# A two-stage kernel (RWKV-style attention, then a squared-ReLU MLP): one hand-held list that orders all engines and transfers is replaced by another

## The chip, the cores and the metric

The kernel runs on one NeuronCore of one Trainium2 chip. The metric is the device time of one execution in microseconds (us). The kernel before takes 181.06 us, the median of 3 runs (181.05 to 181.49). Engine names in the profile: PE is TensorE's matmul, PEld its weight load, DVE VectorE, ACT ScalarE, POOL GpSimd, SP SyncE, which issues all DMAs here.

## What is computed

Inputs are r, k, v, w of shape (4 batches, 8 heads, 768 tokens, 48), u of (8, 48), and two weight matrices. The reference, cut down:

```
for t in range(768):                       # attention, per batch b and head h
    y[t]  = r[t] @ (state + outer(u * k[t], v[t]))
    state = w[t][:, None] * state + outer(k[t], v[t])
x = y.transpose(0, 2, 1, 3).reshape(3072, 384)
h = x @ w_in                               # 384 -> 2048
g = maximum(h, 0) ** 2
out = g @ w_out                            # 2048 -> 384, float32
```

## The kernel before

**Tiling.** The 4 x 768 tokens are cut into 12 steps of 256 tokens (3 steps for a batch; the state is carried inside a batch). Each step has two chunks of 128 tokens. For each step s the kernel does an attention part and an MLP part; an operation's name in the list carries the step and then its part, so `m1_.4.7` is the eighth piece of the first MLP matmul of step 4.

**Attention part of step s.** Four loads, `ld.s.w`, `.k`, `.r`, `.v` (384 KB each, L178). `ww_` multiplies the decays of two neighbouring tokens (L264), `lw_` takes the logarithm on ACT (L268), `cum_` sums logarithms on PE into the PSUM tile `att` (L324 to L328), `al_` (DVE, L333) makes the second sum out of the first in steps 3 to 11, `exp_` and `ac_` exponentiate on ACT (L340, L346). `rw_`, `kw_`, `ku_`, `qp_` prepare products of r, k, w, u (L286, L290, L297, L302), `q_` is a DVE reduction (L307), `qs_`, `v_`, `vs_` are casts and moves (L277, L272). `rd_.s.0` and `rd_.s.1` (DVE, L358 and L361) write the decayed r and k into `rdec_buf` and `kdec_buf`. Their transposes rT and kT are made in steps 0 to 3 by PE (`tr_`, L374) with a copy by DVE or ACT (`rkt_`, L389 and L391), and from step 4 on by a DMA transpose (`dtr_`, L398 and L401). `p_` is the score matmul (L418), `pm_` its masking on DVE (L429 where the scores lie in two single banks, L432 where they lie in an `att` tile), `su_`, `ts_`, `sn_` make the next state (PE L444, DVE or ACT L452/L454, POOL L459), `y_` and `yc_` are the output matmuls (L481, L491), `vq_` (L316) and `ysb_` (DVE, L502) finish y. `yt_` with `xt_` (PE L514, then a copy, L519), or a DMA transpose `dyt_` (L523), give the transposed input xT of the MLP.

**MLP part of step s.** `m1_.s.0` to `.7` (PE, L534) are six matmuls each, into one of four PSUM banks (`bk` 0 and 1, `m1` 0 and 1; the number behind the colon). `rl_` (ACT L543 or DVE L545) empties the bank with ReLU into `gt`; `sq_` squares four pieces at a time (ACT L551 or DVE L553). `m2_.s.c.q` (PE, L562) are four matmuls that add into one bank per chunk c, `os_` (ACT L569 or DVE L571) empties it, `store.s.c` writes 192 KB out (L575). The weights come in eight loads of 768 KB, `ld.0.i` to `ld.3.i` for w_in (L188) and `ld.0.o` to `ld.3.o` for w_out (L194), and are cast to bf16 by `cast.i.*` and `cast.o.*` (L200) on ACT, DVE or POOL.

**What sets the order.** A single string, `ORDER`, of 865 words. The kernel walks it from front to back, and each word issues its instructions; nothing is reordered after that, so each engine's queue, and SP's queue of DMAs, is the string with the other engines' words left out. A word says which engine does the operation where there is a choice (`=A`, `=V`, `=G` for ACT, DVE, POOL) and which PSUM bank it gets (behind the colon). Dependencies between engines, and the reuse of buffers and banks, become semaphore waits; an engine that waits holds everything behind it in its queue. Buffers are few: 4 of each raw input, 4 stage buffers for weights, 3 of `gt`.

`warm_.n.b` issues n matmuls of 512 columns on zeros (L579) that nothing reads; there are 46 of them, all before the first `m1_`.

Of the kernel before, what the change touches and what calls it, by code (L numbers as in the profile page):

```python
# [22 lines left out]
rkt_.1.1=A vs_.1.0=A lw_.2 v_.1=G y_.0:0 yc_.0.1 p_.1.1:1 p_.1.0:m warm_.6.1 vq_.0=G pm_.1.1 cum_.2:1 vs_.1.1=A
pm_.1.0 qs_.1=A exp_.2 warm_.4.1 su_.1:m kw_.2=G ysb_.0=V rw_.2=G ts_.1.0=V y_.1:0 rd_.2.1 yc_.1.0 rd_.2.0
yt_.0:1 xt_.0=V sn_.1.0 cast.i.1=A vq_.1=G ts_.1.1=V tr_.2.1:2 yc_.1.1 ld.2.v tr_.2.0:0 m1_.0.3:1 rkt_.2.1=A
m1_.0.2:2 ac_.2 ysb_.1=V yt_.1:3 rkt_.2.0=A sn_.1.1 p_.2.1:1 rl_.0.3=A cast.i.0=V p_.2.0:0 xt_.1=A ku_.2=V
m1_.0.1:0 vs_.2.1=G m1_.1.0:3 m1_.1.2:1 vs_.2.0=A rl_.0.1=A m1_.1.1:0 v_.2=G rl_.0.2=A rl_.1.0=A rl_.1.2=A
qp_.2=G pm_.2.1 pm_.2.0 su_.2:1 rl_.1.1=V ts_.2.0=V ld.2.i m1_.0.0:2 m1_.1.3:1 cast.i.2=A y_.2:1 q_.2 yc_.2.0
sn_.2.0 yc_.2.1 rl_.1.3=A m1_.0.5:3 ld.3.i m1_.1.5:1 ld.3.w m1_.0.4:0 rl_.0.0=A rl_.0.5=V qs_.2=A rl_.1.5=A
cast.i.3=G m1_.1.7:3 ld.0.o m1_.1.4:1 vq_.2=V ysb_.2=V rl_.0.4=A rl_.1.7=A ww_.3=G cast.o.0=G m1_.0.7:2 yt_.2:3  # L30
ld.2.o m1_.0.6:0 lw_.3 cast.o.2=G cum_.3:1 xt_.2=V rl_.0.7=V ld.3.o m1_.2.4:3 rl_.0.6=V sq_.0.1=A ld.1.o
sq_.0.0=A rl_.1.4=A m1_.2.2:2 sq_.0.2=A m1_.1.6:0 m1_.2.7:1 ld.3.r rl_.1.6=A sq_.1.1=A rl_.2.2=V rl_.2.4=V
m1_.2.5:2 rl_.2.7=V ld.3.k al_.3 rl_.2.5=V cast.o.1=V m1_.2.6:0 m2_.0.1.0:3 m2_.0.1.2 sq_.1.3=V kw_.3=G
m1_.2.3:1 sq_.1.0=A ld.3.v ld.5.w m2_.0.0.0:2 ac_.3 ld.4.w ld.4.r sq_.0.3=A rl_.2.6=A exp_.3 vs_.3.1=G ld.4.v
ld.4.k m1_.2.0:0 m2_.0.0.2 m2_.0.1.1 cast.o.3=V rl_.2.0=A m1_.2.1:0 rw_.3=V m2_.0.1.3 sq_.2.3=A rl_.2.1=A
sq_.1.2=A rl_.2.3=A rd_.3.0 m2_.0.0.1 os_.0.1=A tr_.3.0:0 rd_.3.1 m2_.0.0.3 tr_.3.1:1 ku_.3=V m2_.1.0.1:3
os_.0.0=A m2_.1.0.0 rkt_.3.0=V rkt_.3.1=V p_.3.0:0 v_.3=G sq_.2.1=A su_.3:1 sq_.2.2=A vs_.3.0=A qp_.3=V ld.5.k
p_.3.1:b ts_.3.0=A m2_.2.0.1:2 m2_.1.0.3 m2_.2.0.3 m2_.1.0.2 sq_.2.0=A ww_.4=G pm_.3.0 lw_.4 q_.3 qs_.3=A
cum_.4:0 m2_.2.0.0 ld.6.w v_.4=A pm_.3.1 ww_.5=G rw_.4=G sn_.3.0 ts_.3.1=V vq_.3=G ac_.4 al_.4 m2_.2.0.2
yc_.3.1:1 y_.3 m2_.2.1.0:1 m2_.2.1.2 os_.1.0=A kw_.4=V lw_.5 ysb_.3=V sn_.3.1 store.0.0 os_.2.0=A exp_.4 kw_.5=G  # L40
rd_.4.1 rd_.4.0 cum_.5:1 ac_.5 yt_.3:3 vs_.4.1=G xt_.3=A ld.5.r vs_.4.0=A al_.5 store.0.1 ld.6.r m2_.2.1.3
m2_.2.1.1 os_.2.1=V m1_.3.0:3 rl_.3.0=A exp_.5 su_.4:0 m1_.3.1:2 rl_.3.1=A m2_.1.1.3:0 m2_.1.1.1 dtr_.4.1
ku_.4=V qp_.4=V rw_.5=V m1_.3.7:2 rl_.3.7=A m1_.3.6:1 ts_.4.0=V dtr_.4.0 rl_.3.6=A m2_.1.1.2 m1_.3.5:3 rd_.5.1
rl_.3.5=A m1_.3.4:1 sn_.4.0 ts_.4.1=V p_.4.0:0 q_.4 rd_.5.0 qs_.4=A ww_.6=G vq_.4=G rw_.6=G p_.4.1:1 sq_.3.0=V
m2_.3.1.0:3 m2_.1.1.0 pm_.4.0 yc_.4.1:0 yc_.4.0 sq_.3.3=A m1_.3.3:2 rl_.3.4=A sq_.3.2=A pm_.4.1 y_.4 lw_.6
m1_.3.2:1 rl_.3.3=A rl_.3.2=A cum_.6:1 m2_.3.0.2:2 m2_.3.0.3 sq_.3.1=A m2_.3.1.3 m2_.3.1.1 ku_.5=G qp_.5=G
ld.5.v ysb_.4=V al_.6 ld.7.w ld.6.k ww_.7=G yt_.4:1 m2_.3.1.2 m2_.3.0.0 exp_.6 ac_.6 os_.1.1=V sn_.4.1 m2_.3.0.1
kw_.6=V rd_.6.0 rd_.6.1 dtr_.5.1 ld.6.v v_.5=G dtr_.5.0 xt_.4=A p_.5.1:1 store.2.0 ld.7.r vs_.5.1=A os_.3.1=A
lw_.7 su_.5:b p_.5.0:0 q_.5 v_.6=A store.2.1 ts_.5.0=V m1_.4.1:1 ku_.6=G rl_.4.1=A vs_.6.0=A m1_.4.3:0 os_.3.0=A
pm_.5.0 pm_.5.1 rl_.4.3=V m1_.4.2:3 rl_.4.2=A vs_.6.1=A qs_.5=G m1_.4.4:1 sn_.5.0 yc_.5.1:0 yc_.5.0 rl_.4.4=V  # L50
su_.6:1 dtr_.6.0 m1_.4.7:3 rl_.4.7=A vs_.5.0=G dtr_.6.1 y_.5 m1_.4.6:1 ts_.6.0=V sn_.6.0 ld.9.w m1_.4.5:3
m1_.4.0:2 vq_.5=V sq_.4.1=A rl_.4.6=A rl_.4.5=A sq_.4.2=A ysb_.5=V ts_.6.1=V rl_.4.0=V sq_.4.0=V yt_.5:0
m2_.4.1.1:1 xt_.5=A qp_.6=G q_.6 qs_.6=G ld.7.k p_.6.0:1 ld.8.v yc_.6.1:0 ld.7.v ld.8.r p_.6.1:m store.1.1
ld.8.w vq_.6=G ku_.7=G pm_.6.1 sq_.4.3=A kw_.7=G m2_.4.1.0 m2_.4.1.2 m1_.5.1:0 rl_.5.1=A pm_.6.0 m2_.4.1.3
sn_.6.1 m1_.5.0:2 cum_.7:1 y_.6 m1_.5.7:3 vs_.7.0=A rl_.5.0=A os_.4.1=A ww_.9=V al_.7 m2_.4.0.0:0 rl_.5.7=V
m1_.5.2:2 m1_.5.6:1 ww_.8=G rw_.7=G exp_.7 ac_.7 m2_.4.0.1 vs_.7.1=G m2_.4.0.2 m1_.5.3:3 rl_.5.2=A sq_.5.0=A
v_.7=A rl_.5.3=A m1_.5.5:2 sq_.5.1=A ysb_.6=V vs_.8.0=G m2_.4.0.3 lw_.8 rl_.5.6=A rd_.7.1 qp_.7=V rd_.7.0
sq_.5.3=A su_.7:0 v_.8=G rl_.5.5=V rw_.8=V m1_.5.4:3 rl_.5.4=V m2_.5.1.0:2 cum_.8:1 sq_.5.2=A ts_.7.0=V al_.8
q_.7 m2_.5.1.1 m2_.5.1.3 store.1.0 ld.8.k ld.11.k ac_.8 store.3.1 dyt_.6 dtr_.7.1 dtr_.7.0 exp_.8 kw_.8=V
sn_.7.0 ts_.7.1=V m1_.6.2:3 m2_.5.1.2 m1_.6.3:1 ld.9.r ld.10.w sn_.7.1 os_.4.0=A rd_.8.1 m1_.6.1:0 os_.5.1=A  # L60
ku_.8=G m1_.6.7:2 rd_.8.0 rl_.6.2=V ld.9.k rl_.6.3=A qs_.7=A m1_.6.4:1 su_.8:1 rl_.6.7=A p_.7.1:m p_.7.0:0
qp_.8=G rl_.6.1=V ts_.8.0=V yc_.7.1:1 yc_.7.0 rl_.6.4=A sq_.6.1=A m2_.5.0.2:0 m1_.6.6:1 store.3.0 rl_.6.6=A
sq_.6.3=A dtr_.8.1 pm_.7.1 pm_.7.0 lw_.9 dtr_.8.0 m2_.5.0.1 m1_.6.5:2 y_.7 m1_.6.0:3 m2_.5.0.3 m2_.5.0.0
store.4.1 ku_.9=G q_.8 qs_.8=G ww_.10=G rl_.6.5=V vq_.7=V rl_.6.0=A vs_.8.1=A rw_.9=G sq_.6.0=A p_.8.0:m
p_.8.1:0 kw_.9=G qp_.9=G ysb_.7=V cum_.9:1 m2_.6.0.1:1 ld.9.v ld.10.k os_.5.0=A m2_.6.0.3 m2_.6.1.3:0 m2_.6.0.0
sq_.6.2=V m2_.6.0.2 m2_.6.1.0 sn_.8.0 al_.9 exp_.9 pm_.8.0 rd_.9.0 pm_.8.1 dyt_.7 v_.9=A ac_.9 m1_.7.7:2 y_.8:0
yc_.8.1 rd_.9.1 su_.9:1 vs_.9.1=A yc_.8.0 rl_.7.7=A m1_.7.4:3 ld.10.v vq_.8=G ysb_.8=V m1_.7.0:2 lw_.10
store.4.0 q_.9 rl_.7.4=A ts_.9.0=A rl_.7.0=A cum_.10:0 al_.10 vs_.9.0=V exp_.10 m2_.6.1.1 os_.6.0=V m2_.6.1.2
os_.6.1=A m1_.7.5:2 m1_.7.6:3 m1_.7.2:0 kw_.10=G ld.11.w dtr_.9.0 kw_.11=V qs_.9=G rl_.7.5=A ld.10.r dyt_.8
sq_.7.2=A m1_.7.3:2 m1_.7.1:1 rl_.7.6=A dtr_.9.1 m1_.8.5:3 rl_.7.3=A rl_.7.1=A m1_.8.6:2 v_.10=G sn_.9.0  # L70
ts_.9.1=V rw_.10=G rd_.10.1 rd_.10.0 ac_.10 ku_.11=G rl_.7.2=A rl_.8.5=V sq_.7.1=A ld.11.v m1_.8.7:1 p_.9.0:1
p_.9.1:0 m1_.8.1:3 ww_.11=G store.6.1 vq_.9=G ld.11.r vs_.10.1=G store.6.0 pm_.9.0 sn_.9.1 rl_.8.6=A rl_.8.7=A
rl_.8.1=A lw_.11 m2_.7.1.2:0 m2_.7.1.1 pm_.9.1 m1_.8.3:2 y_.9:0 yc_.9.1 su_.10:1 ysb_.9=V dtr_.10.0 m1_.8.4:1
sq_.7.3=A sq_.7.0=A cum_.11:0 m2_.7.1.3 m2_.7.1.0 ts_.10.0=V rw_.11=V rl_.8.4=A rl_.8.3=V dtr_.10.1 ku_.10=G
sq_.8.2=A os_.7.1=A m1_.8.0:1 m2_.7.0.0:3 m2_.8.1.2:2 m1_.8.2:0 m2_.7.0.1 m2_.7.0.3 m2_.7.0.2 al_.11 exp_.11
rd_.11.1 rd_.11.0 vs_.11.1=G v_.11=G ac_.11 rl_.8.0=A sq_.8.0=A yc_.10.0:0 rl_.8.2=V qp_.10=G p_.10.1:b sn_.10.0
vs_.10.0=G ts_.10.1=V q_.10 qs_.10=G store.7.1 dyt_.9 yc_.10.1 p_.10.0:1 m2_.8.1.0 pm_.10.0 qp_.11=G sn_.10.1
# [17 lines left out]
def kernel(  # L95
# [481 lines left out]
    def warm_(n, i):  # L577
        for _ in range(n):
            nc.tensor.matmul(quad[i][:] if i < 4 else att[i - 4][:, 0, :], warm[:, 0:C], warm[:],  # L579
                             start=True, stop=True)  # L580
# [52 lines left out]
```

## Time and profile before

| | before |
|---|---|
| median of 3 runs | 181.06 us |
| span of the profiled execution | 178.8 us |
| what lies around the span (median less span) | 2.3 us |
| PE busy | 171.0 us (96%) |
| PEld busy | 123.9 us (69%) |
| DVE busy | 138.0 us (77%) |
| ACT busy | 133.4 us (75%) |
| POOL busy | 108.0 us (60%) |
| DMA queue of SP | 35.46 MB, 84.6% of 16 engines' span |
| granted TensorE clock | 1.0 in every slice |

One profiled execution gives the spans; the profile's times are counted from the span's start. In a row of the timeline the columns are start, duration, engine, line, operation, output and inputs, count, and in square brackets how long the engine had been idle before it and what it had waited for. In a row of the chain of waits they are start, duration and what ran. Matmuls are pipelined and the ends of the profile's matmuls are modelled, so PE's busy time hides short waits inside it. A DMA issue is marked SPq; the data land some microseconds later.

### The profile page before, as it was taken

Reading aid. Unit: us, or ns where it says so; the run is one execution under the profiler, and the core shown is the slowest. Engines: PE = TensorE matmul, PEld = TensorE weight load, DVE = VectorE, ACT = ScalarE, POOL = GpSimd, SP = SyncE. Lnnn points to the kernel's source line nnn. Section 1 sums busy time; section 2 is a strip of 40 time slices with the busy share of each in tenths; the row PEclk is TensorE's granted clock in tenths of the full one; section 3 lists DMA queues with packets and bytes.
Section 4 is the critical chain, followed back from the end, with each engine's and each line's share of the span. In section 5 each row is a group of like instructions: output and inputs, shape, how many; then the busy total and the mean of one; then the engine's idle time right before and its main releaser. Section 6 shows DMA issues by size and latency. Waiting matters only on the chain.

```text
span 178.8 us, 5697 instructions
## 1 busy us (share of the span) xinstructions
PE 171.0 (96%) x2383; PEld 123.9 (69%) x2385; DVE 138.0 (77%) x204; ACT 133.4 (75%) x238; POOL 108.0 (60%) x132
## 2 busy tenths in 40 slices
...
GB/s 144 268 263 252 259 346 361 344 368 260 266 243 237 191 216 185 290 166 259 273 291 151 213 255 224 222 175 245 226 79 148 55 48 40 127 12 88 88 44 88
DMA packets 78952, 35.81 MB, mean 200 GB/s; under 512 B 72144, under 2 KB 77392, under 8 KB 78928
## 3 DMA queue, kind: packets, MB, share of 16 engines
q1 hardware_dynamic: 78928, 35.46, 84.6%
...
q14 instruction: 6, 0.05, 0.1%
...
## 4 chain that ended last, share of the span: by engine, by line
PE 56%; POOL 16%; DMA 10%; DVE 9%; issue 4%; SPq 3%; ACT 1%; POOLq 0%; ACTq 0%; DVEq 0%
PE m L562 16%; PE bk L534 11%; PE m L534 11%; PE bk L562 10%; DMA k_raw<-in_k_dram 7%; POOL ku L297 3%; DMA kT<-kdec_buf 3%; POOL r_raw L286 2%; SPq L178 2%; POOL ku L302 2%; DVE pmT L432 2%; PE att L418 2%; POOL ku L316 2%; POOL S L459 2%; DVE y_sb L502 2%
## 5 line engine op out<-in xcount | busy, mean ns | idle before, releaser
L534 PEld LDWEIGHTS <-wi_sb 128*128 128x128 bf16 x576 | 54.9, 98 | 10.7 <-ACT wi_sb L200 0.6
L562 PEld LDWEIGHTS <-gt 128*128 128x128 bf16 x384 | 36.7, 98 | 20.6
L534 PE MATMUL m<-xT,wi_sb 128*128 128x256 bf16 x306 | 40.2, 273 | 0.1
L551 ACT ACTIVATE gt<-gt 128x1024 bf16<-128x1024 f16 x37 | 38.1, 1051 | 0.5
L534 PE MATMUL bk<-xT,wi_sb 128*128 128x256 bf16 x270 | 35.8, 273 | 0.4 <-ACT wi_sb L200 0.4
L562 PE MATMUL bk<-wo_sb,gt 128*128 128x384 bf16 x192 | 35.6, 326 | 0.0
L562 PE MATMUL m<-wo_sb,gt 128*128 128x384 bf16 x192 | 35.0, 326 | 0.0
L543 ACT ACTIVATE gt<-m 128x512 f16<-128x512 f32 x33 | 19.4, 595 | 11.5 <-PE m L534 11.2
L543 ACT ACTIVATE gt<-bk 128x512 f16<-128x512 f32 x35 | 20.6, 596 | 7.2 <-PE bk L534 6.9
L545 DVE TENSOR_SCALAR gt<-m 128x512 f16<-128x512 f32 x18 | 12.3, 688 | 13.1 <-PE m L534 12.4
L432 DVE TENSOR_TENSOR pmT<-att,mask 128x1024 bf16<-128x1024 f32 x16 | 19.1, 1218 | 1.9 <-PE att L418 1.8
L316 POOL TENSOR_TENSOR ku<-v_sh,qs 128x768 f32<-128x768 bf16 x9 | 13.3, 1475 | 10.6 <-ACT qs L277 10.5
L459 POOL TENSOR_TENSOR S<-t_state,ac_buf 128x192 bf16<-128x192 f32 x20 | 12.2, 610 | 8.2 <-DVE t_state L454 5.5
L297 POOL TENSOR_TENSOR ku<-k_raw,u_bc 128x768 f32<-128x768 f32 x9 | 16.7, 1854 | 0.2 <-DMA k_raw<-in_k_dram 0.2
L502 DVE TENSOR_TENSOR y_sb<-att,ku 128x768 bf16<-128x768 f32 x12 | 11.5, 955 | 4.4 <-POOL ku L316 2.0
L290 POOL TENSOR_TENSOR k_raw<-k_raw,w_raw 128x384 f32<-128x384 f32 x8 | 8.1, 1012 | 10.9 <-DMA k_raw<-in_k_dram 10.9
L361 DVE TENSOR_TENSOR kdec_buf<-k_raw,att 128x768 bf16<-128x768 f32 x12 | 11.4, 950 | 3.7 <-ACT att L340 3.7
L277 ACT CAST v_sh<-v_raw 64x384 bf16<-64x384 f32 x26 | 13.2, 509 | 0.3
L302 POOL TENSOR_TENSOR ku<-ku,r_raw 128x768 f32<-128x768 f32 x7 | 12.7, 1811 | 0.2
L358 DVE TENSOR_TENSOR rdec_buf<-r_raw,att 128x384 bf16<-128x384 f32 x24 | 12.3, 547 | 0.6 <-POOL r_raw L286 0.4
L277 POOL CAST v_sh<-v_raw 64x384 bf16<-64x384 f32 x18 | 10.0, 556 | 3.3 <-DMA v_raw<-in_v_dram 2.0
L307 DVE TENSOR_REDUCE q<-ku 128x16 f32<-128x768 f32 x12 | 11.3, 944 | 0.0
...
## 6 DMA issues: line engine op xcount, KB each, us to landing
...
```

The costliest lines, as they stand in the source:

```text
L277: copy(out[j * Q:(j + 1) * Q, c], src[c * Q:(c + 1) * Q, :, j])
L297: tensor_mul("ku_", s, h)(tiles["ku", s][:, hs], raw["k", s][:, hs, 1:3, :], u_bc[:, hs, None, :].to_broadcast([C, n, 2, D]))
L302: tensor_mul("qp_", s, h)(ku, ku, raw["r", s][:, heads(h), 0:2, :])
L316: tensor_mul("vq_", s)(vq[:], tiles["vs", s][:], tiles["qs", s][:, :, :, None].to_broadcast([C, 2, H, D]))
L358: nc.vector.tensor_mul(rdec[0][:, ps, j, :, 0:D], x[:, :, j, :].rearrange("p (a e) d -> p a e d", e=2), dec.rearrange("p (a e) d -> p a e ...
L432: nc.vector.tensor_mul(pmT, ps_p[:].rearrange("p e (x t) -> p (e x) t", t=C), mk.to_broadcast([C, 8, C]))
L459: nc.gpsimd.tensor_mul(t[:], tiles.pop(("ts", s, c))[:].rearrange("p (a d) -> p a d", a=HP), tiles["a_c", s][:, :, c, None].to_broadcast([ ...
L502: nc.vector.tensor_add(tiles["ysb", s][:, x].rearrange("p c (a e d) -> p (c a) e d", e=2, d=D), tiles["y", s][:, :, cols].rearrange("p e ( ...
L534: nc.tensor.matmul(ps1[:, j, :], wi_sb[:, n // 4, kk, n % 4 * 128:(n % 4 + 1) * 128], tiles["xT", s][:, :, kk, :], start=(kk == 0), stop=( ...
L543: nc.scalar.activation(rl, m1, AF.Relu, scale=RS)
L551: nc.scalar.activation(gt, rl, AF.Square)
L562: nc.tensor.matmul(m2, gt[:, 4 * q + n, c * C:(c + 1) * C], wo_sb[:, 4 * q + n, :], start=(summed[s, c] == 1 and n == 0), stop=(summed[s, ...
```

## The change

The string `ORDER` is replaced by another with the same 865 operations on the same data; the number of columns, matmuls, casts and DMAs stays. What differs is the order of the words, the bank numbers, and the engine letter of some words. Counted over the whole list:

| words | engines before | engines after |
|---|---|---|
| `ww_` | DVE 3, POOL 9 | DVE 6, POOL 6 |
| `rw_` | DVE 4, POOL 8 | DVE 5, POOL 7 |
| `qp_` | DVE 5, POOL 7 | DVE 6, POOL 6 |
| `vq_` | DVE 3, POOL 9 | DVE 4, POOL 8 |
| `v_` | ACT 5, POOL 7 | ACT 2, DVE 1, POOL 9 |
| `vs_` | ACT 13, DVE 2, POOL 9 | ACT 10, DVE 2, POOL 12 |
| `qs_` | ACT 7, POOL 5 | ACT 6, POOL 6 |
| `xt_` | ACT 4, DVE 2 | DVE 6 |
| `cast` | ACT 2, DVE 3, POOL 3 | ACT 2, DVE 4, POOL 2 |
| `rl_` | ACT 68, DVE 28 | ACT 76, DVE 20 |
| `sq_` | ACT 37, DVE 11 | ACT 36, DVE 12 |
| `os_` | ACT 19, DVE 5 | ACT 16, DVE 8 |

The function `warm_` gets a third argument that it does not use. The diff, cut to its core (the string has three lines less, so the line numbers below it fall by 3: L531 after is L534 before):

```
 ORDER = """
-ld.0.w ld.0.k ld.0.r ld.0.u ld.1.w ww_.0=V lw_.0 warm_.11.5 cum_.0:0 kw_.0=G exp_.0 rd_.0.1 ld.0.v warm_.8.5
...
+ld.0.w warm_.2.4.5 ld.0.k ld.0.r warm_.11.2.0 ld.0.u ld.1.w ld.0.v ww_.0=V lw_.0 ld.1.k cum_.0:0 kw_.0=V warm_.4.1.8
...
-    def warm_(n, i):
+    def warm_(n, i, x=0):
         for _ in range(n):
```

Two places of it are used below.

SP's queue behind the last w_in load, rows 18 to 25 of before (`w_raw` of step 3, the four w_out loads of `ld.0.o`, `ld.2.o`, `ld.3.o`, `ld.1.o`, then r, k, v of step 3; `w_st` is the stage buffer of a weight):

```order
L178 DMA w_raw_805<-in_w_dram 128x8x96
L194 DMA w_st_828<-in_moe_w_out_dram 128x4x384
L194 DMA w_st_857<-in_moe_w_out_dram 128x4x384
L194 DMA w_st_875<-in_moe_w_out_dram 128x4x384
L194 DMA w_st_886<-in_moe_w_out_dram 128x4x384
L178 DMA r_raw_909<-in_r_dram 128x8x96
L178 DMA k_raw_922<-in_k_dram 128x8x96
L178 DMA v_raw_950<-in_v_dram 128x8x96
```

The same place after (w, r, k of step 3, `ld.0.o`, w of step 4, v of step 3, then `ld.3.o`, `ld.2.o`, `ld.1.o`):

```order
L175 DMA w_raw_515<-in_w_dram 128x8x96
L175 DMA r_raw_578<-in_r_dram 128x8x96
L175 DMA k_raw_629<-in_k_dram 128x8x96
L191 DMA w_st_720<-in_moe_w_out_dram 128x4x384
L175 DMA w_raw_767<-in_w_dram 128x8x96
L175 DMA v_raw_777<-in_v_dram 128x8x96
L191 DMA w_st_804<-in_moe_w_out_dram 128x4x384
L191 DMA w_st_880<-in_moe_w_out_dram 128x4x384
L191 DMA w_st_890<-in_moe_w_out_dram 128x4x384
```

Four loads of attention data now stand between the w_in loads and most of w_out: `ld.2.o` was the sixth load behind `ld.2.v`, and is now the tenth.

DVE's queue from the first w_out cast on it to the state update `ts_.3.1` (`t_state`), before (`gt` rows are `rl_` and `sq_`, `rT` and `kT` the copies `rkt_.3.0` and `rkt_.3.1`):

```order
L200 CAST wo_sb<-w_st 128x1536
L553 TENSOR_TENSOR gt<-gt 128x1024
L200 CAST wo_sb<-w_st 128x1536
L286 TENSOR_TENSOR r_raw<-r_raw,w_raw 128x8x48
L358 TENSOR_TENSOR rdec_buf_109<-r_raw,att_87 128x4x2x48 x2
L361 TENSOR_TENSOR kdec_buf_110<-k_raw,att_87 128x16x48
L297 TENSOR_TENSOR ku<-k_raw,u_bc 128x768
L389 COPY rT<-bk_88 128x1024
L391 COPY kT<-bk_89 128x1024
L302 TENSOR_TENSOR ku<-ku,r_raw 128x768
L432 TENSOR_TENSOR pmT<-att_86,mask 128x1024
L307 TENSOR_REDUCE q<-ku 128x16
```

The last part of the same stretch after, from `q_.3` to `ts_.3.1`, with `cast.o.2` and `cast.o.1` in it:

```order
L304 TENSOR_REDUCE q<-ku 128x16
L197 CAST wo_sb<-w_st 128x1536
L388 COPY kT<-bk_88 128x1024
L542 TENSOR_SCALAR gt<-bk_89 128x512
L197 CAST wo_sb<-w_st 128x1536
L429 TENSOR_TENSOR pmT<-att_87,mask 128x1024
L426 TENSOR_TENSOR pmT<-bk_88,mask 128x512
L426 TENSOR_TENSOR pmT<-bk_89,mask 128x512
L451 TENSOR_TENSOR t_state<-S,att_86 128x192
```

The casts of `ld.2.o` and `ld.1.o` now stand on DVE between `q_.3` and the copy, masks and state update of step 3; before, DVE had the casts of `ld.1.o` and `ld.3.o`, ahead of step 3's `rd_`.

141 lines of the change are left out of this document (69 added, 72 removed).

## The prediction

> **What bounds the kernel now.** I read the page first, then the busy times in six stretches, then the chain of waits at both ends, then each engine's timeline around the first `m1_`. The page's first row says that PE leads.
>
> ```profile
> PE 171.0 (96%) x2383; PEld 123.9 (69%) x2385; DVE 138.0 (77%) x204; ACT 133.4 (75%) x238; POOL 108.0 (60%) x132
> ```
>
> The stretches (from:to, its length, then busy time and count of PE, PEld, DVE, ACT, POOL, then clock, DMA share, GB/s) say where.
>
> ```profile
> 0.00:26.00 26.00, 21.98 (x324) 12.14 (x326) 20.53 (x36) 17.41 (x36) 19.30 (x30) 1.00 1.02 253
> 26.00:52.00 26.00, 25.90 (x311) 21.09 (x312) 22.19 (x29) 24.39 (x41) 16.00 (x17) 1.00 1.10 314
> 52.00:100.00 48.00, 47.99 (x760) 34.98 (x759) 44.84 (x65) 42.30 (x78) 34.59 (x43) 1.00 1.01 221
> 100.00:145.00 45.00, 44.70 (x755) 33.57 (x753) 37.07 (x58) 34.05 (x59) 36.62 (x44) 1.00 0.94 182
> 145.00:175.43 30.43, 30.41 (x241) 22.08 (x238) 13.35 (x20) 14.79 (x26) 1.48 (x1) 1.00 0.21 67
> 175.43:178.80 3.37, 0.00 (x0) 0.00 (x0) 0.00 (x0) 0.49 (x1) 0.00 (x0) 1.00 0.18 63
> ```
>
> Before 26 us PE idles 4.0 us and spends the rest on warm-up matmuls and the first attention steps. From 26.00 to 175.43 it idles only 0.10 + 0.01 + 0.30 + 0.02 = 0.43 us, and the last 3.37 us are one `os_`, one store and the program's end. So the time is the start (26.0), PE's work behind it (149.4), the tail (3.4), and 2.3 us around the span to the median of 181.06. The DMA share stays near 1 until 145 us: DMA is the other full resource, and DVE and ACT are near full to 100 us.
>
> The chain of waits ends as the table does:
>
> ```profile
> 173.46 1.96 PE bk L562 x12
> 175.50 0.49 ACT o_sb L569
> ```
>
> **The change part by part.** *The start.* The first `m1_` waits for the cast of `ld.1.i`, and the cast for the DMA, as ACT's and PE's timelines show:
>
> ```profile
> 24.50 1.47 ACT L200 CAST wi_sb<-w_st 128x1536 bf16<-128x1536 f32 x1 [1.57 <-DMA w_st<-in_moe_w_in_dram]
> ```
>
> ```profile
> 26.02 0.83 PE L534 MATMUL bk<-xT,wi_sb 128*128 128x256 bf16 x6 [0.39 <-ACT wi_sb L200]
> 26.93 0.82 PE L534 MATMUL m<-xT,wi_sb 128*128 128x256 bf16 x6
> ```
>
> `ld.1.i` is the 13th load in both lists behind the same bytes, and PE's list up to the first `m1_` holds the same words in another order. I cost the start at nothing. What must stay covered: 13 warm-up matmuls now stand ahead of `cum_.0`, where there were 11, and DVE takes `kw_.0` and `rw_.0` from POOL.
>
> ```profile
> 1.19 4.87 PE L579 MATMUL att<-warm 128*128 128x512 bf16 x11 [1.19 <-DVE half_ones L228]
> ```
>
> ```profile
> 7.66 0.95 DVE L361 TENSOR_TENSOR kdec_buf<-k_raw,att 128x768 bf16<-128x768 f32 x1 [2.47 <-ACT att L340]
> 9.99 0.80 DVE L264 TENSOR_TENSOR ww<-w_raw 128x384 f32<-128x384 f32 x1 [0.45 <-DMA w_raw<-in_w_dram]
> 24.93 0.55 DVE L519 COPY xT<-bk 128x768 bf16<-128x768 bf16 x1
> ```
>
> Two more at 4.87 / 11 = 0.44 each delay `cum_.0` by up to 0.9, and with it DVE's `rd_`. `kw_.0` and `rw_.0` fit into the 2.47 us in which DVE idled. Of the 0.9, 0.45 goes into DVE's wait for the second w load, and xT is done at 25.48, 0.5 ahead of the cast's end at 25.97: just covered; without that cover it would be up to 0.5 late.
>
> *The second `m1_`* started at 26.93, not at 26.02 + 0.66 = 26.68, since its bank was still being copied out, as the chain shows; two plain neighbours follow 0.66 apart.
>
> ```profile
> 25.88 1.01 ACT kT L391
> 26.93 0.82 PE m L534 x6
> 27.75 0.33 PE m L514 x6
> 28.08 0.58 PE att L418 x32
> 28.66 0.76 PE bk L534 x6
> 29.42 0.66 PE m L534 x6
> ```
>
> After, `m1_.0.2` gets bank 3, which DVE emptied long before: **-0.25**.
>
> *Changes of form.* The `m1_` behind a 64-row group (L418) takes 0.76, not 0.66: 0.10 for leaving the group, and I allow as much again, unseen here, for entering. The new list has 23 runs of `p_`, `su_`, `yc_` in place of 25: 0.2 to 0.4 saved; I take **-0.3**.
>
> *The stretch to `cum_.4`.* Between the first `m1_` and `cum_.4` PE has the same words in both lists (24 `m1_`, 4 `p_` and so on) but 7 `m2_` where there were 14. An `m2_` takes 1.96 / 3 = 0.65, so PE comes to `cum_.4` 4.55 earlier than here:
>
> ```profile
> 56.01 0.24 PE L324 MATMUL att<-half_ones,lw_buf 128*128 128x2 bf16 x4
> ```
>
> That is 56.01 - 4.55 - 0.25 = 51.2. `cum_.4` writes the bank that `ts_.3.1` reads, and `ts_.3.1` now stands on DVE behind `cast.o.2`, which needs `ld.2.o`. When does that land? POOL's waits give landings:
>
> ```profile
> 28.36 1.05 POOL L277 CAST v_sh<-v_raw 64x384 bf16<-64x384 f32 x2 [2.03 <-DMA v_raw<-in_v_dram]
> 35.89 1.84 POOL L200 CAST wo_sb<-w_st 128x1536 bf16<-128x1536 f32 x1 [0.36 <-DMA w_st<-in_moe_w_out_dram]
> 37.99 1.47 POOL L200 CAST wo_sb<-w_st 128x1536 bf16<-128x1536 f32 x1 [0.26 <-DMA w_st<-in_moe_w_out_dram]
> 45.08 1.01 POOL L290 TENSOR_TENSOR k_raw<-k_raw,w_raw 128x384 f32<-128x384 f32 x1 [5.62 <-DMA k_raw<-in_k_dram]
> ```
>
> One weight load (37.99 - 35.89) is 2.1. Two weights, r and k follow in 45.08 - 37.99 = 7.09, so one 384 KB load is 1.45. The queue is full throughout, so landings add up: from `ld.2.v` at 28.3 to `ld.2.o` there are now 5 weights and 5 small loads, 10.5 + 7.25, landing at 46.0 (by the same sum `ld.0.o` of before lands at 36.0, and its cast began at 35.89). What stands on DVE from `cast.o.2` until `ts_.3.1` is done, at the means of the groups (busy us and mean ns behind the bar; the cast's are min/median/max):
>
> ```profile
> L200 DVE CAST wo_sb<-w_st x2: 951/1358/1766, 43.7 to 45.1; 128x1536 bf16<-128x1536 f32 x2
> ```
>
> ```profile
> L432 DVE TENSOR_TENSOR pmT<-att,mask 128x1024 bf16<-128x1024 f32 x16 | 19.1, 1218 | 1.9 <-PE att L418 1.8
> L545 DVE TENSOR_SCALAR gt<-bk 128x512 f16<-128x512 f32 x10 | 6.8, 687 | 0.7 <-ACT gt L543 0.6
> L429 DVE TENSOR_TENSOR pmT<-bk,mask 128x512 bf16<-128x512 f32 x4 | 2.6, 679 | 0.0
> L454 DVE TENSOR_TENSOR t_state<-S,att 128x192 f32<-128x192 bf16 x12 | 4.2, 347 | 1.1 <-POOL S L459 0.7 <-PE att L444 0.4
> L391 DVE COPY kT<-bk 128x1024 bf16<-128x1024 bf16 x1 | 0.7, 675 | 0.0
> ```
>
> ```profile
> 20.81 1.28 DVE L429 TENSOR_TENSOR pmT<-m,mask 128x512 bf16<-128x512 f32 x2
> ```
>
> Two casts, copy, `rl_`, 1.22, 2 x 0.68, 0.35: 6.2 with the short cast, 7.0 with the median one. Neighbours overlap by about 0.08 (the two of 0.68 in the last row span 1.28), so 5.6 to 6.4. DVE's work from xT's end at 25.48 to the end of `ts_.3.1` at 57.27 was, in before:
>
> ```profile
> 25.48:57.27 31.79, 31.32 (x408) 24.39 (x406) 27.98 (x37) 30.09 (x53) 18.41 (x20) 1.00 1.06 299
> ```
>
> 27.98 busy. The new list has 5 `rl_` (0.69), a `ku_` and a `rw_` less there, and a `vs_`, a `ww_`, an `xt_` and a cast more; I put that at 2 us less, an estimate from their groups: 26.0, of which 20 lie ahead of `cast.o.2`. DVE comes to it at 45.5 and waits 0.5 for the 46.0. Then `ts_.3.1` is done at 51.6 to 52.4, against PE's 51.2. PE waits 0.4 to 1.2; 0 to 0.7 if `ld.2.o` lands half a microsecond earlier. I take **+0.7**. All later work of PE stands behind `cum_.4`, so this is lost for good.
>
> *Later.* PE idled 0.30 us from 100 to 145 in before, in waits whose neighbours all move; I take **-0.05**, between all of it gone and as much come anew. The tail has the same form (`os_` on ACT, one store): nothing. Sum: -0.25 - 0.3 + 0.7 - 0.05 = **+0.1, so 181.2 us**; by the bounds of the terms alone -0.9 to +1.0, that is 180.2 to 182.1.
>
> **The rivals.** *Faster: no wait at `cum_.4`.* If the loads come half a microsecond earlier and the casts are short ones, the 0.7 falls away and the rest stays: 181.06 - 0.25 - 0.3 - 0.05 = 180.5, and 180.1 with 0.4 for the runs and all 0.30 of the old waits gone; I price it at 180.3. For it: DMA moved 314 GB/s from 26 to 52 us against 253 before that, and attention data come earlier than before, which takes pressure off POOL. Against: casts beside POOL's work were long ones.
>
> *Slower: the course of transfers is late, at `cast.o.2`.* Every microsecond that `ld.2.o` lands behind 46.0 goes through DVE to `cum_.4` one for one. If the ten loads take a tenth longer (17.75 x 0.1), that is 1.8 more: 183.0. For it: POOL's 5.62 us of waiting for `k_raw` in the last row of the landings show that data, not engines, set the pace there. Against: the sum fits the landings of before to 0.1.
>
> *Slower: DVE and POOL hold each other up.* DVE gets more work that reads and writes SBUF only. What such a meeting costs is seen where DVE's `ku_` ran beside POOL's `ww_`, and once alone:
>
> ```profile
> 49.40 1.78 DVE L297 TENSOR_TENSOR ku<-k_raw,u_bc 128x768 f32<-128x768 f32 x1
> 62.24 0.95 DVE L297 TENSOR_TENSOR ku<-k_raw,u_bc 128x768 f32<-128x768 f32 x1
> ```
>
> ```profile
> 49.37 2.67 POOL L264 TENSOR_TENSOR ww<-w_raw 128x384 f32<-128x384 f32 x2 [0.43 <-DMA w_raw<-in_w_dram]
> ```
>
> That is 0.83 for a meeting. Ahead of `cast.o.2` DVE's 0.5 us of waiting hide a little of it; behind it stand two casts, so 2 x 0.83 in place of the median's 2 x 0.4: +0.9, 182.1, if both meet POOL; and with more of them by step 6, where DVE is still 93% busy (44.84 of 48), as much again: 182.5. [...]
>
> That the change does not do what it says can be left aside: the two queues shown above differ as stated.
>
> **How the numbers follow.** About the same as forecast, 0.40; faster, 0.25; late transfers, 0.20; DVE against POOL, 0.15. A measurement of this kernel can tell 0.3%, 0.54 us, from no change. The forecast's own range gives 0.31 within, 0.03 faster, 0.06 slower; the faster rival 0.23 faster, 0.02 within; the late transfers 0.19 slower, 0.01 within; the last 0.14 slower, 0.01 within. Together: faster 0.26, within 0.35, slower 0.39. The range reaches from 179.8 (181.06 - 0.25 - 0.4 - 0.43, all that PE idled behind 26 us, and 0.2 more for waits that the modelled ends hide) to 183.4 (the late transfers' 183.0 and half of the last rival's 0.9); the likeliest case's own is 180.2 to 182.1.
>
> **What would show it.** In the profile after: the first `m1_` at 26.0 and the next 0.66 behind it; DVE idle before a w_out cast, for DMA, near 45.5 to 46 us, and PE idle before L321 (`cum_`) near 51 to 52; PE otherwise busy to within half a microsecond until the tail of 3.4. A first `m1_` later than 26.3 breaks the first step; no DVE wait before the cast breaks the sum of landings; a PE idle time of over 1 us elsewhere, before L415 (`p_`) for a transpose above all, means that I looked at the wrong place.

## The result, and the profile after

Side by side on one chip, the kernel after takes 186.51 us (median of 4 runs, 186.16 to 187.05), the kernel before 181.10 us (4 runs, 181.05 to 181.49): a ratio of 1.0299, with a 95% interval of 1.0275 to 1.0322. It is slower by 5.4 us, far outside the range given. The profiled execution took 187.05 us with a span of 185.2 us, 6.4 us longer than the span of before (178.8); the medians differ by 5.4. (Executions of the experiments that stood apart from the others of their kernel, two of them at 435 and 963 us, are left out of the ratios below.)

The same stretches as in the prediction (from:to, length, then busy time and count of PE, PEld, DVE, ACT, POOL, clock, DMA share, GB/s), after:

```profile
26.00:52.00 26.00, 24.82 (x364) 20.63 (x362) 22.63 (x33) 23.26 (x42) 17.58 (x20) 1.00 1.08 309
52.00:100.00 48.00, 45.23 (x653) 33.21 (x652) 40.71 (x60) 36.86 (x70) 40.59 (x42) 1.00 1.14 245
100.00:145.00 45.00, 42.69 (x697) 31.45 (x696) 38.29 (x59) 33.15 (x57) 29.12 (x49) 1.00 0.77 150
145.00:181.00 36.00, 36.00 (x352) 26.35 (x350) 18.88 (x29) 14.07 (x21) 1.76 (x2) 1.00 0.27 68
```

PE did the same work, but idled 1.18, 2.77 and 2.31 us in the first three stretches where it had idled 0.10, 0.01 and 0.30. That is 6.26 against 0.41: nearly the whole difference of the spans. The first 26 us and the last 3.4 us (the last `m2_` ends near 181.8) are as before.

PE's waits after, from the view of waits (engine, what it writes, its line; what it waited for; total us, times, longest):

```profile
PE att L415 <- DMA kT<-kdec_buf: 1.8, 1, 1.8
...
PE m L415 <- DMA rT<-rdec_buf: 1.1, 1, 1.1
PE m L531 <- ACT gt L540: 1.0, 2, 0.6
...
PE m L531 <- DMA xT<-y_sb: 0.6, 1, 0.6
PE att L321 <- DVE t_state L451: 0.5, 1, 0.5
...
PE m L559 <- DVE wo_sb L197: 0.4, 1, 0.4
```

Three are for operands that a DMA transpose brings: kT of `dtr_.5.1` for `p_.5.0`, rT of `dtr_.8.0` for `p_.8.0`, xT of `dyt_.7` for `m1_.7.6`; 3.5 us together. In before, no `p_` can have waited longer than 0.3 us, since PE idled no more than that in any of these stretches. The chain of waits shows the first of them, from the issue of a store on (SPq is a DMA issue):

```profile
69.69 0.46 SPq L572
...
70.20 4.99 DMA w_raw<-in_w_dram
75.19 5.79 DMA kT<-kdec_buf
...
81.02 0.65 PE att L415 x32
```

`rd_.5.1` on DVE had written kdec_buf at 67.43 + 0.95 = 68.4, but its transpose was issued at 75.19 and landed at 80.98, because of what stands ahead of it in SP's queue.

```profile
67.43 0.95 DVE L358 TENSOR_TENSOR kdec_buf<-k_raw,att 128x768 bf16<-128x768 f32 x1
```

That queue after (start of the issue, its length, line, transfer):

```profile
66.37 0.56 SPq L175 DMA_DIRECT2D k_raw<-in_k_dram  x1
67.04 2.49 SPq L395 DMA_TRANSPOSE rT<-rdec_buf  x1
69.62 0.53 SPq L572 DMA_DIRECT2D out_dram<-o_sb  x1
70.20 0.42 SPq L175 DMA_DIRECT2D w_raw<-in_w_dram  x1
70.72 1.60 SPq L175 DMA_DIRECT2D v_raw<-in_v_dram  x1
72.41 1.14 SPq L175 DMA_DIRECT2D k_raw<-in_k_dram  x1
73.64 1.46 SPq L572 DMA_DIRECT2D out_dram<-o_sb  x1
75.19 1.71 SPq L398 DMA_TRANSPOSE kT<-kdec_buf  x1
```

And the same two transposes in before:

```profile
65.88 4.06 SPq L401 DMA_TRANSPOSE kT<-kdec_buf  x1
69.99 0.57 SPq L178 DMA_DIRECT2D v_raw<-in_v_dram  x1
70.67 1.47 SPq L398 DMA_TRANSPOSE rT<-rdec_buf  x1
```

One load stood between them there; now it is two stores and three loads, with the load of step 8's k (66.37) ahead of both. It is not this place alone. Read from the trace in this way, the transposed operand of each pair that lands last (DVE has written it, SP issues its transpose, it lands; us):

| operand | before: written, issued, landed | after: written, issued, landed |
|---|---|---|
| step 5 (`dtr_.5.0`, after `dtr_.5.1`) | 67.8, 70.7, 74.7 | 68.4, 75.2, 81.0 |
| `dtr_.6.1` | 77.1, 77.6, 80.9 | 78.1, 84.1, 87.6 |
| `dyt_.6` | 92.7, 92.8, 96.1 | 94.9, 96.1, 101.1 |
| `dtr_.7.0` | 96.4, 96.4, 100.3 | 100.8, 101.0, 106.4 |
| `dtr_.8.0` | 102.5, 103.8, 109.3 | 106.0, 107.5, 112.2 |
| `dyt_.7` | 110.3, 110.3, 113.1 | 111.7, 111.7, 117.6 |

Step by step, they land 3 to 7 us later, but not all of it is lost in SP's queue. In steps 5 and 6 it mostly is: `dtr_.5.1` and `dtr_.6.1` were issued 6.8 and 6.0 us after their operand was written. `dtr_.7.0`, `dtr_.8.0` and `dyt_.7` were issued 0.2, 1.5 and 0.0 us after it, about as in before; DVE wrote these operands 4.4, 3.5 and 1.4 us later, and `dyt_.7` was then 5.9 us under way in place of 2.8. How much of DVE's lateness goes back to the wait of step 5, and how much to the new order of the engines, this trace does not tell.

The loads that stand ahead are also taken up earlier by the engines: the first use of `ld.8.k` moved from 99.8 us to 72.6, of `ld.6.v` from 78.3 to 59.5, of `ld.8.w` from 93.1 to 83.0, of `ld.8.r` from 96.9 to 85.4, of `ld.10.r` from 121.7 to 105.8, of `ld.11.v` from 130.4 to 110.8 (some others moved back, by 1 to 8 us). For `ld.8.k` the timelines show it, on DVE in before and on POOL after:

```profile
99.82 0.55 DVE L290 TENSOR_TENSOR k_raw<-k_raw,w_raw 128x384 f32<-128x384 f32 x1
```

```profile
72.56 1.82 POOL L294 TENSOR_TENSOR ku<-k_raw,u_bc 128x768 f32<-128x768 f32 x1 [0.17 <-DMA k_raw<-in_k_dram]
```

At the same time PE has less of its own work ahead of these operands: counted in the two lists from the first `m1_` on, 39 `m2_` and 5 `su_` ahead of the first `m1_.6` where there were 43 and 6, and 44 `m2_` and 55 `m1_` ahead of `p_.8.0` where there were 48 and 56. At 0.65 us for an `m2_`, 0.66 for an `m1_` and 0.37 for a `su_` that is 3.0 and 3.3 us less; the work is left for the end. Both meet in two stretches, cut where the last load, `ld.11.r`, lands (before 122.60 + 5.6 = 128.2, after 125.68 + 3.9 = 129.6):

```profile
26.00:128.20 102.20, 101.89 (x1505) 77.62 (x1506) 91.50 (x129) 90.81 (x162) 74.93 (x86) 1.00 1.05 248
128.20:175.43 47.23, 47.10 (x560) 34.08 (x557) 25.95 (x40) 24.72 (x42) 13.75 (x18) 1.00 0.38 79
```

```profile
26.00:129.60 103.60, 97.34 (x1436) 73.75 (x1434) 87.07 (x129) 81.52 (x148) 78.80 (x94) 1.00 1.07 242
129.60:181.80 52.20, 52.20 (x629) 38.22 (x627) 33.44 (x50) 26.27 (x42) 10.25 (x17) 1.00 0.32 78
```

On average DMA is full (share 1.05 and 1.07) until the last load lands, and that comes only 1.4 us later. But by then PE has done 97.3 us of work instead of 101.9, and has 52.2 left instead of 47.2. 1.4 + 5.0 is the 6.4; this is the loss booked by time, not yet its cause. The average hides a pause in after, for which before has no counterpart: from 116.4 to 119.7 nothing was under way, since SP stood at the transpose `dtr_.9.1`, whose operand DVE wrote at 118.5.

```profile
116.00:120.00 4.00, 3.17 (x34) 1.99 (x31) 3.73 (x7) 2.72 (x6) 0.85 (x1) 1.00 0.12 25
```

### The profile page after: what moved, and what is told of

It reads as the page before. It is cut to its first block, busy times and chain, and to the rows that moved or that the text cites. A ratio compares the mean times of both kernels' runs of the same rounds, so it can differ in the third digit from the quotient of the medians.

```text
span 185.2 us, 5702 instructions
## 1 busy us (share of the span) xinstructions
PE 171.0 (92%) x2382; PEld 124.0 (67%) x2385; DVE 141.6 (76%) x214; ACT 125.8 (68%) x225; POOL 106.2 (57%) x137
## 4 chain that ended last, share of the span: by engine, by line
PE 52%; DMA 22%; SPq 11%; DVE 4%; POOL 4%; ACT 3%; issue 2%; DVEq 0%; ACTq 0%; POOLq 0%
PE bk L559 13%; PE m L531 12%; PE m L559 11%; PE bk L531 10%; SPq L175 8%; DMA w_st<-in_moe_w_in_dram 6%; DMA rT<-rdec_buf 5%; DMA w_st<-in_moe_w_out_dram 5%; DMA kT<-kdec_buf 3%; DMA w_raw<-in_w_dram 3%; PE att L415 1%; PE att L478 1%; PE att L488 1%; ACT gt L540 1%; DVE rdec_buf L355 1%
## 5 line engine op out<-in xcount | busy, mean ns | idle before, releaser
L531 PEld LDWEIGHTS <-wi_sb 128*128 128x128 bf16 x576 | 55.2, 98 | 12.4 <-issue 2.0
L531 PE MATMUL m<-xT,wi_sb 128*128 128x256 bf16 x324 | 42.4, 273 | 1.9 <-ACT gt L540 1.0
L559 PE MATMUL bk<-wo_sb,gt 128*128 128x384 bf16 x224 | 42.5, 326 | 0.0
L540 ACT ACTIVATE gt<-m 128x512 f16<-128x512 f32 x41 | 23.9, 598 | 15.2 <-PE m L531 15.0
L531 PE MATMUL bk<-xT,wi_sb 128*128 128x256 bf16 x252 | 33.4, 273 | 0.0
L559 PE MATMUL m<-wo_sb,gt 128*128 128x384 bf16 x160 | 30.1, 326 | 0.4 <-DVE wo_sb L197 0.4
L429 DVE TENSOR_TENSOR pmT<-att,mask 128x1024 bf16<-128x1024 f32 x14 | 16.8, 1215 | 0.0
L274 POOL CAST v_sh<-v_raw 64x384 bf16<-64x384 f32 x24 | 13.2, 551 | 1.0
L542 DVE TENSOR_SCALAR gt<-m 128x512 f16<-128x512 f32 x13 | 8.9, 687 | 4.6 <-PE m L531 4.1
L269 POOL CAST v_bf<-v_raw 128x768 bf16<-128x768 f32 x9 | 9.7, 1082 | 4.6 <-DMA v_raw<-in_v_dram 4.5
L415 PEld LDWEIGHTS <-kT 64*64 64x64 bf16 x384 | 6.3, 106 | 6.8 <-DMA kT<-kdec_buf 2.2
```

Source lines behind the costliest of these rows:

```text
L274: copy(out[j * Q:(j + 1) * Q, c], src[c * Q:(c + 1) * Q, :, j])
L429: nc.vector.tensor_mul(pmT, ps_p[:].rearrange("p e (x t) -> p (e x) t", t=C), mk.to_broadcast([C, 8, C]))
L531: nc.tensor.matmul(ps1[:, j, :], wi_sb[:, n // 4, kk, n % 4 * 128:(n % 4 + 1) * 128], tiles["xT", s][:, :, kk, :], start=(kk == 0), stop=( ...
L540: nc.scalar.activation(rl, m1, AF.Relu, scale=RS)
L559: nc.tensor.matmul(m2, gt[:, 4 * q + n, c * C:(c + 1) * C], wo_sb[:, 4 * q + n, :], start=(summed[s, c] == 1 and n == 0), stop=(summed[s, ...
```

## The experiments

The first four asked where the loss sits: transposes too far back in SP's queue (the first theory), the new engine choices (the second), or w_out loads that come late for `cum_.4` (the third).

**One transpose ahead.** SP's queue of after, one word moved:

```
-dtr_.5.0 store.1.0 ld.7.w ld.7.v ld.7.k store.2.1 dtr_.5.1 store.2.0
+dtr_.5.0 dtr_.5.1 store.1.0 ld.7.w ld.7.v ld.7.k store.2.1 store.2.0
```

> The new order with one word moved: dtr_.5.1 stands right behind rd_.5.1, so SP issues it ahead of store.1.0, ld.7.w, ld.7.v, ld.7.k and store.2.1, not behind them. Theory 1 (the time went to transposes that queue behind loads and stores which need not go first): kT of step 5 lands about 5 us earlier, PE's wait of 1.9 us ahead of p_.5.0 goes, 184.6 us (184.3 to 185.2). Theory 2 (the engine letters are the cause: DVE and POOL hold each other up, so everything is late): rd_.5.1 is itself late, the wait comes back elsewhere, 186.2 or more. Theory 3 (the late w_out loads set the lateness): the wait behind 75 us is repaid later, about 186.

Measured: 187.1 us (186.05 to 187.76), before 180.7; ratio 1.0341 (1.0291 to 1.0391). The wait for kT of step 5 is gone, yet no time came back. PE's timeline shows where it went: to the next transposed operand, `dyt_.6`, for which after had waited 0.3 us by its matmul starts.

```profile
100.33 0.83 PE L531 MATMUL m<-xT,wi_sb 128*128 128x256 bf16 x6 [1.88 <-DMA xT<-y_sb]
```

The queue is the reason there: `ysb_.6` had written the operand at 92.4, and SP issued its transpose at 95.5. But as a single misplaced word, the first theory fell.

**More transposes ahead.** On top of that:

```
-store.1.1 store.4.0 store.4.1 dtr_.8.1 dtr_.8.0 ld.10.k store.0.0 ld.10.v dyt_.7
+dtr_.8.1 dtr_.8.0 store.1.1 store.4.0 store.4.1 dyt_.7 ld.10.k store.0.0 ld.10.v
```

> As the one before, and at two more places transposes go ahead of transfers that nobody waits for soon: dtr_.8.1 and dtr_.8.0 ahead of store.1.1, store.4.0 and store.4.1, and dyt_.7 ahead of ld.10.k, store.0.0 and ld.10.v. Theory 1: the waits of 1.9 (p_.5), 1.15 (p_.8) and 0.75 (m1_.7) go or shrink to half, 182.5 to 184. Theories 2 and 3: no more than e1_dtr5 gives, since the producers are late.

Measured: 189.14 us (187.77 to 190.85), ratio 1.0434 (1.038 to 1.0488). The three waits of after are gone but for 0.2 us, and yet it is slower than after. Its trace has 1.98 us before `m1_.6` for `dyt_.6`, as in the run before, and a new wait of 2.67: `ld.10.v`, now behind `dyt_.7`, came late for ACT's `vs_.10.0`, and behind that in ACT's queue stands the `rl_` that frees PE's bank.

```profile
120.88 1.03 ACT L274 CAST v_sh<-v_raw 64x384 bf16<-64x384 f32 x2 [2.44 <-DMA v_raw<-in_v_dram]
```

**The load of step 3's v behind the w_out loads.**

```
-ld.0.o ld.4.w ld.3.v ld.3.o ld.2.o ld.1.o
+ld.0.o ld.4.w ld.3.o ld.2.o ld.1.o ld.3.v
```

> The new order with ld.3.v moved behind ld.1.o, so that the last three w_out loads land one small load (1.45 us) earlier. Theory of the prediction (DVE held at cast.o.2 by the landing, PE at cum_.4): DVE's wait of 1.35 us before cast.o.2 goes, PE's 0.7 us before cum_.4 shrinks to 0 to 0.3, time 185.8 to 186.2. Theory 3 in its strong form (late w_out loads set the lateness of all that follows): 1.4 us or more, 185.1 or less. Theory 1: the wait before p_.5.0 stays or grows, 186 to 187.

Measured: 188.15 us (187.04 to 188.53), ratio 1.0395 (1.034 to 1.045). The wait at `cum_.4` grew instead of going:

```profile
PE att L321 <- DVE t_state L451: 1.8, 1, 1.8
```

DVE no longer waits for the cast's data, but step 3's own v stands on the same path: POOL's `v_.3` now waits for it, and behind that on POOL stands the state product `sn_.3.0`, for which `ts_.3.1` waited 2.12 us.

```profile
49.20 1.15 POOL L269 CAST v_bf<-v_raw 128x768 bf16<-128x768 f32 x1 [3.67 <-DMA v_raw<-in_v_dram]
```

So nothing is won by putting this load behind the weights. The third theory is not borne out, but not tested cleanly either, since the edit put a second wait in place of the first.

**The order of after with the engine choices of before** (124 words get their old letter, no word moves):

```
-kw_.6=G ... ww_.7=V ... xt_.4=V ... rl_.4.4=A
+kw_.6=V ... ww_.7=G ... xt_.4=A ... rl_.4.4=V
```

> The new order with the engine letters of before (124 words change their engine). Theory 2 (letters): the loss goes, 181 to 183 us. Theory 1 (place of the transfers): SP's queue is the same, PE still waits over 1 us before p_.5.0 and before p_.8, 185 us or more; it may be slower than the changed kernel, since the order was not made for these letters.

Measured: 197.94 us (197.5 to 199.2), ratio 1.0957 (1.0907 to 1.1007). The loss does not go with the new choices: with the old ones the new order is far slower, with PE's waits spread over ACT and DVE. The counterpart, **the order of before with the choices of after**, was run later:

> The order before on every queue, with only the 124 engine choices of the order after (the counterpart of the run of the order after with the choices of before, 197.9 us). Theory T says nothing of the choices by themselves except that they fit the order that they were searched with: slower than before, 185 to 200 us, with PE waiting for ScalarE, VectorE and GpSimd. [...]

Measured: 208.34 to 209.37 us in three runs, ratio 1.1541 (1.1502 to 1.1579), above the 185 to 200 expected. An order and its choices belong together, and neither half of the change can be timed by itself; these two runs do not clear the choices of a part in the loss.

From here on the theory (T) was the one of the last section: transfers and PE's work ahead of each transposed operand set the pace, over the whole stretch from 60 to 120 us. First, **loads with long slack put off**, in SP's queue of after (with `dtr_.5.1` ahead as in the first run):

```
-... ld.8.r ld.11.w dtr_.6.0 ... ld.9.r ld.9.k ld.9.v ld.10.r dyt_.6 ld.10.w dtr_.7.1 dtr_.7.0 ld.11.v ...
+... ld.8.r dtr_.6.0 ... ld.9.k ld.10.r dyt_.6 ld.10.w dtr_.7.1 dtr_.7.0 ld.9.r ld.9.v ld.11.v dtr_.8.1 dtr_.8.0
+store.1.1 store.4.0 store.4.1 ld.10.k store.0.0 ld.10.v dyt_.7 ld.11.w
```

> The order after, with the transpose dtr_.5.1 right behind its producer rd_.5.1 (as in the first experiment), and with transfers that nobody needs soon moved behind transposed operands: ld.9.r and ld.9.v (needed at 114.7 and 113.6 us of the order after, landed at 96.2 and 99.0) behind dtr_.7.0, ld.11.w (needed at 126.2, landed at 86.0) behind dyt_.7, and three stores behind dtr_.8.0. Theory T (the transfers that run ahead of each transposed operand set the pace between 60 and 120 us): dtr_.6.0, dtr_.6.1 land 2.1 us earlier, dyt_.6 and dtr_.7 about 5 us earlier, dtr_.8 about 3.7; the waits before p_.5.0 (1.9), m1_.6 (2.0 in the first experiment) and p_.8.0 (1.15) shrink to under 0.5 each; median 183.5 us, 182.5 to 185. Rival E (the engines between the transposes, with their new letters, are late themselves, whatever the queue holds): the same time as after, 186 to 187.5, with the waits before the same matmuls, put down to ScalarE, VectorE or GpSimd.

Measured: 186.96 to 189.02 us in three runs, ratio 1.0386 (1.0321 to 1.045). The expectation missed. (It also takes 2.1 us for a w load; that is a weight's price. In after, `ld.11.w` landed at 86.0, 1.5 behind the r load ahead of it, so a w load costs about what the 1.45 of the prediction has for the others.) `dyt_.6` and `dtr_.7` did land 4.3 and 3.4 us earlier, and their waits went; but the loads put behind `dtr_.7` stood ahead of `dtr_.8.0`, which landed at 112.4 as in after, and PE, there earlier than before, waited all the longer:

```profile
112.49 0.43 PE L415 MATMUL m<-rT,kT 64*64 64x128 bf16 x16 [2.96 <-DMA rT<-rdec_buf]
```

**Transfers left out.** The order after, with ten loads less; steps 7 to 11 read w and v of step 6:

```
+            if part in "vw" and s > 6:
+                raw[part, s] = raw[part, 6]
+                return
+            pool = consts if part in "vw" and s == 6 else a_in
```

> The order after, with ten loads left out: the steps 7 to 11 read w and v of step 6 from a buffer of their own, so that the output of these steps is not the reference's, and all work on the engines stays. By 2.1 us a load of w and 1.43 us one of v in the queue of after that takes 17.6 us of transfers away, 3.5 of them ahead of dtr_.5.1, 8.4 or more ahead of dyt_.6. Theory T: the waits before p_.5.0 (1.9 us), p_.8.0 (1.15) and m1_.7 (0.75) go, those ahead of 60 us (about 2 us together) stay; median 182.5 us, 181.8 to 183.5. Rival E: the engines' own order sets the pace, 185.5 to 187.

Measured: 183.23 us (181.92 to 184.2), ratio 1.0124 (1.0066 to 1.0182), against 1.0299 for after: 3.2 us of the 5.4 come back, by the two intervals 2 to 4 (at about 1.4 us a load, an estimate from the same landings, 14 us of transfers were left out, not 17.6). PE's waits from 26 us to the end of its work, all that the view shows (four lines are added to the code, so L535 is `m1_`):

```profile
PE m L535 <- ACT gt L544: 0.8, 1, 0.8
PE bk L535 <- DVE rT L390: 0.7, 1, 0.7
PE att L325 <- DVE t_state L455: 0.5, 1, 0.5
PE att L445 <- DVE kdec_buf L362: 0.3, 1, 0.3
```

None is for a DMA transpose any more. About 1.2% is left, and rival E may hold for that part; it is not free of transfers, though, for the 0.5 us at `cum_.4` (`t_state`) still stands behind a w_out load.

**The same ten loads left out of before.**

> The order before, with the same ten loads left out (the steps 7 to 11 read w and v of step 6, so that their output is not the reference's). PE waits for little there (0.43 us from 26 us to 175.4 us), so both theories expect no more than that: 180.8 us, 180.2 to 181.4. It says what the missing loads are worth where transfers are covered.

Measured: 180.82 us (10 runs, 180.28 to 181.31), ratio 1.0001 (0.9981 to 1.0022). The same transfers are worth about 3 us in after and nothing in before: there they were all covered.

**Five loads ahead, in before.** Nothing but SP's queue changes:

```
-ld.7.w ld.6.k dtr_.5.1 ... dtr_.7.1 dtr_.7.0 ...
+ld.7.w ld.6.k ld.7.k ld.7.v ld.8.k dtr_.5.1 ... dtr_.7.1 ld.11.w ld.10.r dtr_.7.0 ...
```

> The order before on every engine, with five loads moved ahead in the queue of transfers and nothing else: ld.7.k, ld.7.v, ld.8.k ahead of dtr_.5.1 (4.3 us of transfers), ld.11.w and ld.10.r ahead of dtr_.7.0 (3.5 us). Theory T: dtr_.5.0 lands at about 79.0 instead of 74.7, while p_.5 began at 77.3, so 1.7 us of wait; dtr_.8.0 lands 3.5 us after its 109.3 while p_.8 began at 109.94, so up to 2.9 us (less what PE has already lost); median 184 us, 182.5 to 185.5. Rival E: the order of transfers alone costs little since the engines are as before: 181 to 181.8.

Measured: 186.24 us (185.64 to 186.92), ratio 1.0296 (1.025 to 1.0341). That is above the range expected. By five loads moved, the kernel before loses as much as after does; that the two losses are equal is chance, since these are not the moves of after. The two waits stand where they were foreseen, 1.1 us longer and 1.2 us shorter:

```profile
79.97 0.43 PE L415 MATMUL att<-rT,kT 64*64 64x128 bf16 x16 [2.80 <-DMA rT<-rdec_buf]
...
115.18 0.43 PE L415 MATMUL m<-rT,kT 64*64 64x128 bf16 x16 [1.69 <-DMA rT<-rdec_buf]
```

**All places of the queue mended at once**, in after:

```
+dtr_.5.0 dtr_.5.1 ... dtr_.7.1 dtr_.7.0 ld.9.v dtr_.8.1 dtr_.8.0 store.1.1 ld.11.v dyt_.7
+store.4.0 ld.9.r store.4.1 ld.10.k ld.10.v ld.11.w store.0.0
```

> The order after, with the queue of transfers repaired at all three places of its waits at once: dtr_.5.1 right behind rd_.5.1; ahead of dtr_.8.0 no longer ld.9.r, ld.11.v, ld.11.w and two stores (in the last try ld.9.r, ld.9.v and ld.11.v stood between dtr_.7.0 and dtr_.8.1, and dtr_.8.0 still landed at 112.4 us, where PE waited 3.0); ahead of dyt_.7 no longer ld.9.r, ld.10.k, ld.10.v and three stores. Engines as after. Theory T (what runs ahead of a transposed operand sets when PE gets it): dtr_.8.0 lands at about 108, dyt_.7 at about 113.5; the wait before p_.8.0 is under 0.5 us, that before m1_.7 under 1; the loads put off cost GpSimd some waiting for ld.11.v and ld.9.r; median 184.5 us, 183 to 186. Rival E (the engines are late themselves): 186 us or more, with the waits put down to engines.

Measured: 191.46 us (191.3 to 191.64), ratio 1.0589 (1.0563 to 1.0614). The worst of these orders, and its trace shows where the time went. `dtr_.8.0` landed at 110.3 and `dyt_.7` at 114.1, and `p_.8.0` no longer waits. But `ld.10.v`, put off, is needed by ACT's `vs_.10.0`, and behind that in ACT's queue stands the `rl_` that frees PE's bank:

```profile
120.36 1.03 ACT L273 CAST v_sh<-v_raw 64x384 bf16<-64x384 f32 x2 [4.05 <-DMA v_raw<-in_v_dram]
```

```profile
122.13 1.23 PE L530 MATMUL m<-xT,wi_sb 128*128 128x256 bf16 x5 [5.10 <-ACT gt L539]
```

It is the path of the second run again: what moved ahead of one operand made another late.

**The early uses put off with their loads**, in after: `v_.11` and `rw_.10` move on POOL, the loads as above, a little further back.

```
+v_.9 rw_.10 v_.11
+dtr_.7.0 ld.9.v ld.9.r dtr_.8.1 dtr_.8.0 ld.10.w store.1.1 dyt_.7 ld.10.v ld.10.k store.4.0 ld.10.r store.4.1
+ld.11.v ld.11.w store.0.0
```

> The order after, with the early uses of two loads put off together with the loads: GpSimd's v_.11 and rw_.10 (begun at 110.8 and 105.8 us in the order after, in before at 130.4 and 121.7) move behind its v_.9, into a stretch where GpSimd had waited 5 us, and ld.11.v, ld.10.r, ld.11.w, ld.10.k, ld.10.v move behind dyt_.7, ld.9.r, ld.9.v behind dtr_.7.0, ld.10.w behind dtr_.8.0; dtr_.5.1 stands right behind rd_.5.1. Theory T (loads that engines use early stand ahead of the transposes, and in the last try, where only the loads were put off, ScalarE's vs_.10.0 waited 4.0 us for ld.10.v instead): now the transposes and the loads both come in time; dtr_.6.1 lands near 85, dtr_.8.0 near 109, dyt_.7 near 114, ld.10.v near 115.5; PE's waits behind 80 us are under 0.6 each and 1.5 together, the early ones (about 2.7 to 80 us) stay; median 183.6 us, 182.5 to 185. Rival E (the engines' order is late by itself, whatever the transfers do): 186 or more, PE waiting for ScalarE, VectorE or GpSimd that wait for no transfer.

Measured: 185.53 to 188.69 us, median 187.94; too scattered for a ratio, and not better than after. Between 75 and 100 us PE was busy 24.98 of 25.00, so the waits of steps 5 and 6 were cured. Behind 100 us PE waited again, 0.7 us for `dtr_.8.0`, 1.7 for a bank and 1.2 for `dyt_.8`. The bank is freed by ACT's `rl_`, and ahead of that ACT had waited 1.8 us for an output buffer: `os_.5.1` needs the one that `store.1.1` empties, and the edit had put this store back (issued at 108.3, in after at 103.5).

```profile
113.37 0.49 ACT L566 ACTIVATE o_sb<-bk 128x384 f32<-128x384 f32 x1 [1.81 <-DMA out_dram<-o_sb]
```

The loads came late too (POOL waited 4.7 us for one of r), but whether PE paid for that was not followed.

**Less work of PE ahead, in before.** No transfer moves; three `m2_` go from ahead of `p_.8.0` to behind `p_.8.1`:

```
-m2_.5.0.1 ... m2_.5.0.3 m2_.5.0.0 p_.8.0 p_.8.1
+p_.8.0 p_.8.1 m2_.5.0.1 m2_.5.0.3 m2_.5.0.0
```

> The order before with no transfer moved: only TensorE's three m2_.5.0 groups (3 x 0.65 us) go from just ahead of p_.8.0 to just behind p_.8.1. The same work on TensorE, less of it ahead of a transposed operand. Theory T (what counts is the work that TensorE has left ahead of a transpose that lands when it lands): p_.8.0 is reached at about 108.0 us instead of 109.94, its operand of dtr_.8.0 lands at 109.3, so PE waits about 1.4 there and loses it for good: 182.2 us, 181.5 to 182.8. Rival N (the order of TensorE's own work is free as long as it has work): as before, 180.8, 180.4 to 181.2.

Measured: 182.2 us (181.87 to 182.66), before 180.99; ratio 1.0071 (1.0043 to 1.0099). As theory T had it, and not rival N:

```profile
PE m L415 <- DMA rT<-rdec_buf: 1.7, 1, 1.7
```

What the runs show: in before, transfers are covered (ten less gain nothing), but with little to spare. The readers of steps 5 and 8 start here:

```profile
77.30 0.43 PE L418 MATMUL att<-rT,kT 64*64 64x128 bf16 x16
109.94 0.43 PE L418 MATMUL m<-rT,kT 64*64 64x128 bf16 x16
```

Their operands had landed at 74.7 and 109.3, so 2.6 and 0.6 us were to spare, and either more transfers or less of PE's work ahead of these points cost time at once (186.24 and 182.2 us). In after, transfers are not covered; with fewer of them about 3.2 of the 5.4 us return. What they do not show is an order of SP's queue that makes the engine queues of after fast; six tries failed, and whether there is one stays open. The 2.2 us that remain with fewer transfers were not taken apart by runs; the four waits in that run's trace come to 2.3.

## Why the prediction was wrong, point by point

*What bounds the kernel*: right as far as it went. PE leads (96% busy), and DMA is the other full resource (share 0.94 to 1.10 until 145 us); the prediction said so in one clause, and then priced the second at one place only.

*The start*: right. The first `m1_` came at 26.12 and the second 0.65 behind it, with no bank to wait for:

```profile
26.12 0.81 PE L531 MATMUL bk<-xT,wi_sb 128*128 128x256 bf16 x6
26.77 0.82 PE L531 MATMUL m<-xT,wi_sb 128*128 128x256 bf16 x6
```

The 0.1 is the cover named there: xT is now done at 25.51 + 0.55 = 26.06, just behind the weights' cast.

*Changes of form* (-0.3): nothing speaks against it, but it drowns in the waits and is not shown; no run shows the cost of entering a group that it allows; its row shows only the 0.76 us of an `m1_` behind a group against 0.66.

*The stretch to `cum_.4`* (+0.7): the wait came where it was put, by the path that was named, and matmul starts show 0.71 us of it (the view of waits 0.5). Its inner numbers were all late:

```profile
47.65 0.97 DVE L197 CAST wo_sb<-w_st 128x1536 bf16<-128x1536 f32 x1 [1.34 <-DMA w_st<-in_moe_w_out_dram]
```

DVE came to `cast.o.2` at 46.31, not 45.5, and waited 1.34, not 0.5, since `ld.2.o` landed at 47.63 instead of 46.0; the two casts there were short ones (0.97 and 0.96). (In before, `ld.2.o` was the fifth load behind `ld.2.v`, not the sixth; the sum counts the ten of after, and is not touched.) That the size still fitted is luck: PE itself was late, at `cum_.4` at 52.9 and not at 51.2. It had waited 0.57 us near 33 us for a bank that ACT empties (behind a w_in cast that had waited for its load), and 0.6 for a w_out cast near 48, two waits that I had not priced.

*Later* (-0.05): this step failed. It said that PE's waits behind that point had neighbours that all move, and took "between all of it gone and as much come anew" as its bounds, that is 0.3 us either way. Measured, PE idled 4.5 us from 55 us to the end of its work. From an idle time of 0.3 us in before I had read that there was room; it shows only that everything was covered, not by how much. The cover was thin (2.6 us at `p_.5` and 0.6 at `p_.8`; the moved loads and the moved `m2_` show that it is soon used up), and both sides of it moved against the kernel: the transposed operands landed 3 to 7 us later, and PE's work ahead of `m1_.6` and `p_.8.0` shrank by about 3. Seven `m2_` less ahead of `cum_.4` stood in the prediction as PE coming 4.55 us earlier; that the same work was then missing as cover was not drawn from it. Of the 5.4 us this step accounts for about 3.2 by the run with fewer transfers; the cause of the rest stays open.

*The rivals*: late transfers were the right kind of cause, but at `cast.o.2` and with 1.8 us; the place was one that the prediction itself named as the sign of having looked wrongly, a wait of over 1 us before L415 for a transpose. DVE against POOL is a small part as far as was seen: the one meeting found among PE's waits was `kw_.4`, which took 1.72 us on DVE beside POOL's `ku_.5` (59.63 to 61.45; 0.59 for `kw_.5` a little later), and cost 0.37 at `su_.4`. A slip in that rival: with 0.9 twice its price is 183.0, not 182.5. And its example shows that `ku_` took 1.78 us beside POOL and 0.95 alone, not what made it longer; it ended at 51.18, 0.8 behind POOL's first `ww_` (50.37).

```profile
60.15 1.72 DVE L287 TENSOR_TENSOR k_raw<-k_raw,w_raw 128x384 f32<-128x384 f32 x1
```
